# An attention and two-MLP kernel on one core: second terms of weights on VectorE, a key copy cast by its DMA, split steps by heads and earlier loads

## Chip, cores and metric

The kernel runs on one core of a Trainium2 chip. The metric is the device time of one execution in microseconds (us). Before the change the median of three runs is 738.6 us (737.14 to 741.27).

## What is computed

Attention over 2 batches, 8 heads, 576 positions and a head size of 64, with a bias that decays by the running sum of `relu(s)`; then an MLP with 2048 hidden units and a leaky ReLU; then a mixture of 4 experts with 1024 hidden units each, weighted by normalized probabilities. All of it is float32.

```python
scores = scale * (q @ k.T)
cum = cumsum(maximum(s, 0))
scores = where(causal, -1e9, scores + minimum(-(cum[i] - cum[j]), 0))
attn = softmax(scores);  x = (attn @ v) as rows of 512
x = leaky(x @ w_in) @ w_out          # 512 -> 2048 -> 512
p = probs / (sum(probs) + 1e-9)
out = sum_e p[e] * (relu(x @ w1[e]) @ w2[e])
```

## The kernel before

**Two terms.** TensorE multiplies in the type `F32R`, into which a float32 value does not fit whole. Each operand is therefore split into a first term, the value cast to `F32R` (a copy), and a second term, the value less the first (a subtraction). A product takes three matmuls: first by first, second by first, first by second. For a chunk of weights (128 x 1024) `split_w` (line 220) issues both: `nc.scalar.copy` on ACT and, right behind it, `nc.gpsimd.tensor_tensor` with `subtract` on POOL. In the profile these are `w<-raw` on ACT and on POOL.

**Stages.** Tokens fall into two sets. In the first stage (to about 225 us) attention runs as 16 units (`Unit`, line 632), one per batch and pair of heads: units 0 to 7 hold the first 256 positions of each sequence (4 items each, an item is a tile of 128 queries of one head), units 8 to 15 the rest (6 items each). From item 20 on, steps of the first MLP on the first token set are woven in (`main = mlps(phases[0])`). What is left of that MLP ends the first set (to about 250 us); the second set follows with a form of seven products (`seven_steps`, `paired_up`), and from about 373 us the experts.

**Order.** Until `fixed = False` (line 827) every instruction keeps the order in which the Python code issues it, on each engine. `attention()` (line 720) goes through the items with lags: scores of item i, exponentials of item i-1, transposes of i-3, product with the values of i-5, and, at the end of a unit, its finish of i-7. It yields at three places per item, and there the loops at lines 773 and 795 step the other generators: `main` (MLP matmuls), `units_of_w` = `supply()` and `late` = `late_splits()`. In the first half of attention two matmuls of zeros (`idling`) fill TensorE per item.

**Weights.** w_in and w_out come as 64-bit numbers. `supply()` (line 135) turns 16 chunks into float32, in six steps each: one ACT operation and four on DVE (`raw<-raw` twice, `raw<-r,raw` twice, 128 x 1024), writes the chunk to DRAM (`w_f`), and loads the next 1 MB (`r<-in_moe_...`). A chunk that TensorE needs soon is split at once; later ones are loaded again from `w_f` by `late_splits()` (line 118), which loads, yields three times, and splits.

**Keys.** For units 8 to 15 `load_keys` (line 578) loads q (`qr`, twice, for both halves of the partitions) and k (`kr`) on SP's queue; `split_keys` (line 606) makes in three steps, one per item: `qs` (ACT copy, later a DVE subtraction on 64 partitions), `ks` (ACT copy of 64 x 1152, DVE subtraction of 64 x 1152) and `kd` (a second ACT copy of the same first term, beside two rows of the decay that `decay` loads). `kd` and `ks` have two buffers each. The steps for unit 8 begin at the third item of unit 6, those of a later unit n at the third item of unit n-1. The keys of unit 8 are loaded when unit 5 is made, those of unit 9 when unit 7 is made, and of each other unit n when unit n-2 is made.

**End of a unit.** The outputs of a unit gather in `ps_o`, a PSUM pool of one buffer. At its last product DVE makes `st` and `xo` from it, and the next unit's first product has to wait for that. The flag `ending` marks a yield after which DVE shall get no step of `supply()`; it is set at the step of the exponentials only.

Of the kernel before, what the change touches and what calls it, by code (L numbers as in the profile page):

```python
# [13 lines left out]
ALU = mybir.AluOpType  # L14
# [5 lines left out]
def attention_moe_moe2(ctx: ExitStack, tc: tile.TileContext, q, k, v, s, w_in, w_out, probs, w1, w2, out):  # L20
# [10 lines left out]
    fixed = True  # L31
# [19 lines left out]
    B, H, D, S = q.shape  # L51
# [5 lines left out]
    NP = H // 2  # L57
# [17 lines left out]
    def f32(ap):  # L75
        return ap.bitcast(F32)
# [41 lines left out]
    def late_splits():  # L118

        nonlocal reading  # L120
        while len(ready) < CONVERTED:
            n = len(ready)
            if n < min(retired + WB + 2, stored):
                reading, raw = True, load_w(*stream[n][:3])
                yield
                yield
                yield
                while n >= retired + WB:
                    yield
                ready.append(split_w(raw, stream[n][1], False))  # L130
                reading = False
            else:
                yield
# [45 lines left out]
    def seven(raw):  # L179

        steps = seven_steps(raw)
        while True:
            w = next(steps)
            if w is not None:
                return w
# [34 lines left out]
    def split_w(raw, shape, paired):  # L220
        if paired:
            return seven(raw)
        w = wpool.tile([P, 2, 1024], F32R, tag="w", name="w")
        nc.scalar.copy(w[:, 0], raw)
        nc.gpsimd.tensor_tensor(w[:, 1], raw, f32(w[:, 0]), ALU.subtract)
        return w.rearrange("p l (a b) -> p l a b", a=shape[0])

    def up_piece(e, f, c):
# [340 lines left out]
    def of_unit(n):  # L569

        b = n % 2
        i0, i1 = (0, 2) if n < 2 * NP else (2, QT)
        return b, n % (2 * NP) // 2, i0, i1

    units = 4 * NP
    k_raw = {}

    def load_keys(n):

        b, hp, i0, i1 = of_unit(n)  # L580
        q0, q1 = tiles[i0][0], tiles[i1 - 1][2]
        heads = slice(2 * hp, 2 * hp + 2)
        k_of = k[b, heads, :, :q1].rearrange("h d s -> d h s")
        q_of = q[b, heads, :, q0:q1].rearrange("h d s -> d h s")
        if i0 == 0:
            nc.sync.dma_start(k_e[n % 3][:D], k_of)
            nc.sync.dma_start(q_e[n % 3][:D], q_of)
        else:
            qr = ap.tile([P, 2, S // 2 + 32], F32, tag="qr", name="qr")
            for j in range(2):  # L590
                nc.sync.dma_start(qr[j * D : (j + 1) * D], q_of)
            kr = ap.tile([P, 2, S], F32, tag="kr", name="kr")[:D]
            nc.sync.dma_start(kr, k_of)
            k_raw[n] = qr, kr
# [10 lines left out]

    def split_keys(n):

        qr, kr = k_raw.pop(n)
        qs = q_s[n % 2]
        ks, kd = (ap.tile([P, 2, S], F32R, tag=tag, name=tag) for tag in ("ks", "kd"))  # L610
        decay(n, kd)
        nc.scalar.copy(qs[:, 0], qr)
        yield
        nc.vector.tensor_tensor(qs[:D, 1], qr[:D], f32(qs[:D, 0]), ALU.subtract)
        nc.scalar.copy(ks[:D], kr)
        yield
        nc.vector.tensor_tensor(ks[D:], kr, f32(ks[:D]), ALU.subtract)
        nc.scalar.copy(kd[:D], kr)
        k_split[n] = ks, kd, qs
        yield  # L620

    def decay(n, kd):

        b, hp, i0, i1 = of_unit(n)
        q1, h = tiles[i1 - 1][2], b * H + 2 * hp
        if n < 2:
            for l, queue in enumerate((nc.sync, nc.scalar)):
                queue.dma_start(kd[D + l : D + l + 1], f32(cum2[h : h + 2, l, :q1]))
        else:
            nc.sync.dma_start(f32(kd[D:DK, :, :q1]), cum_d[:, h : h + 2, :q1])  # L630
# [84 lines left out]
    ending = False  # L715
# [4 lines left out]
    def attention():  # L720

        nonlocal ending
        items, starts, n = [], {}, 0
        i, split = 0, iter(())
        while n < units or i < len(items) + 7:
            if n < units and i == len(items):
                u = Unit(n)
                starts[n] = i
                items += [(u, *of) for of in u.items]
                if n + 2 < units and n + 2 != 2 * NP:  # L730
                    load_keys(n + 2)
                    if n + 2 < 2 * NP:
                        decay(n + 2, k_e[(n + 2) % 3])
                if n + 3 == 2 * NP:
                    load_keys(n + 3)
                n += 1
            if n < units - 1 and i == starts[n - 1] + 2:
                load_values(n + 1)
            if i == starts[n - 1] + 2 and 2 * NP - 1 <= n < units and n != 2 * NP:
                split = split_keys(max(n, 2 * NP))  # L740
            for step, lag in STEPS:
                if 0 <= i - lag < len(items):
                    u, *of = items[i - lag]
                    ending = step == Unit.exps and 0 <= i - 5 < len(items) and items[i - 5][1:] == items[i - 5][0].items[-1]
                    step(u, *of)
                if lag == 1:
                    next(split, None)
                if lag in (1, 3, 7):
                    yield i
            i += 1  # L750

# [8 lines left out]
    with ExitStack() as phase:  # L760
        x_t[0] = phase.enter_context(tc.tile_pool(name="x0pool", bufs=1)).tile([P, 2, KD, sizes[0]], F32R, name="x0")
        wpool = phase.enter_context(tc.tile_pool(name="wpool", bufs=4))
        r64p = phase.enter_context(tc.tile_pool(name="r64p", bufs=2))

        OPENED = (22, 23, 25, 27, 28, 30, 32, 34, 36)
        side, units_of_w, late, opened = attention(), supply(), late_splits(), 0
        nothing = ps_mm.tile([P, 512], F32, tag="mm", name="nothing")
        with tc.tile_pool(name="early", bufs=1) as early:
            ones = pads(early)
            cumulative()  # L770
            main = mlps(phases[0])

            for at_ in range(3 * 64):
                i = next(side)
                if done == 2 * NP:
                    break
                if at_ % 3 == 0 and i in (6, 8):
                    nc.scalar.copy(q_s[i // 2 - 3][D:DK, 1], ones[D:DK])
                if at_ % 3 == 1:
                    if i < 20:  # L780
                        idling(2)
                    elif opened < len(OPENED) and i >= OPENED[opened] and opened < 3 * (done // 2):
                        next(main)
                        opened += 1
                if at_ % 3 < 2 and i >= 31:
                    onto_held()
                if at_ % 3 == 2:
                    if i in (1, 5):
                        fetch64(i // 4)
                    if i >= 8 and (i < 21 or i >= 29):  # L790
                        next(units_of_w)
        hidden_pool(phase, 6)

        owed = 0
        for at_, i in enumerate(side):
            if at_ % 3 < 2:
                owed += WOVEN * KD / (2.0 * (48 - 6))
                while owed >= 1.0:
                    next(main)
                    owed -= 1.0  # L800
            if at_ % 3 != 1:
                next(late, None)
            if at_ % 3 == 2 or at_ % 3 == 0 and not ending:
                next(units_of_w, None)
        attn.close()
        w7pool = ctx.enter_context(tc.tile_pool(name="w7pool", bufs=2, side="right"))
        scratch = ctx.enter_context(tc.tile_pool(name="scratch", bufs=2, side="right"))
        t7pool = ctx.enter_context(tc.tile_pool(name="t7pool", bufs=1, side="right"))
        tokens = paired_steps(1, x_t[1], t7pool)
        banks.close()  # L810
        ps_mm = ctx.enter_context(tc.tile_pool(name="ps_all", bufs=8, space=PSUM))

        sevens = first_sevens()
        for m, _ in enumerate(main):
            if m % 2 == 0:
                next(late, None)
            if m % 4 == 0:
                next(tokens, None)
            if m % 4 == 2:
                next(units_of_w, None)  # L820
            if m % 4 % 2 and m >= 4:
                next(sevens, None)
        for _ in sevens:
            pass
        for _ in tokens:
            pass
    fixed = False
# [56 lines left out]
```

## Time and profile before

| | |
|---|---|
| runs shown | 738.6, 741.27, 737.14 us |
| profiled execution, its own time | 740.89 us |
| span in the trace, first to last instruction | 739.1 us |
| busy: PE, DVE, ACT, POOL | 715.3, 434.1, 330.9, 288.4 us |
| mean granted clock of TensorE | 0.998 |
| chain that ended last: PE, DVE, ACT | 88%, 5%, 3% |

In the profile, L43 is the helper that records every operation, so groups are told apart by tiles: `out<-in`. "Idle before" is time in which the engine stood still just ahead of the group, with the engine and tile that released it. PE's busy time is modelled from pipelined matmuls; PEld are its weight loads.

### The profile page before, as it was taken

How to read it: one execution, taken by the hardware profiler on the slowest of the kernel's cores; microseconds unless marked ns; L12 is line 12 of the kernel's file. 1: busy time of each engine (PE TensorE's matmuls, PEld its weight loads, DVE VectorE, ACT ScalarE, POOL GpSimd, SP SyncE). 2: the span in 40 equal slices, each digit the busy share in tenths (PEclk: the TensorE clock that was granted, in tenths of full speed). 3: DMA queues.
4: the chain of work that ended last, by engine and by line, in shares of the span. 5: the costliest groups of instructions: out<-in, count | busy, mean ns of one | idle time of the engine just before them, and what ended most of it. 6: DMA issues, size and time to landing. Idle time of an engine off the chain costs nothing.

```text
span 739.1 us, 11479 instructions
## 1 busy us (share of the span) xinstructions
PE 715.3 (97%) x4420; PEld 651.7 (88%) x4420; DVE 434.1 (59%) x866; ACT 330.9 (45%) x643; POOL 288.4 (39%) x234
## 2 busy tenths in 40 slices
PE   9988899899999999999999999999999999999997
PEld 9877788798887899999988988989889898898996
DVE  4848797889736864853874544544446444454442
ACT  5756887687654476453431322413324133132210
POOL 4111121211127969895163272422714327053200
PEclk9999999999999999999999999999999999999999
DMA  6785377675442123131020110201102011010002
GB/s 177 209 196 170 107 218 234 190 250 200 155 161 86 54 92 113 58 114 58 1 86 30 58 57 11 76 29 58 58 0 86 29 58 58 1 58 0 1 38 91
DMA packets 40745, 68.85 MB, mean 93 GB/s; under 512 B 3988, under 2 KB 22964, under 8 KB 40692
## 3 DMA queue, kind: packets, MB, share of 16 engines
q1 hardware_dynamic: 31980, 42.97, 19.2%
q10 hardware_dynamic: 8712, 25.17, 10.0%
q8 instruction: 34, 0.56, 0.3%
q14 instruction: 19, 0.16, 0.1%
HBM read 57.30 MB, written 10.82 MB: 92 GB/s over the span
## 4 chain that ended last, share of the span: by engine, by line
PE 88%; DVE 5%; ACT 3%; issue 2%; DMA 1%; SPq 0%; ACTq 0%; DVEq 0%
PE ps_d L43 40%; PE ps_u L43 34%; PE ps_o L43 5%; PE ps_sc L43 3%; PE ps_pt L43 3%; PE nothing L43 2%; DVE raw L43 2%; DMA qr<-in_q_dram 1%; DVE z L43 1%; DVE t L43 1%; PE ps_x L43 1%; ACT pv L43 1%; ACT ps_u L43 1%; ACT ks L43 0%; ACT ht L43 0%
## 5 line engine op out<-in xcount | busy, mean ns | idle before, releaser
L43 POOL TENSOR_TENSOR w<-raw,w 128x1024 fp32r<-128x1024 f32 (+2 forms) x88 | 148.1, 1701 | 399.4 <-ACT w L43 393.0
L43 PE MATMUL ps_u<-t,w 128*128 128x320 f32 (+1 forms) x1680 | 236.5, 299 | 1.2 <-DVE t L43 1.2
L43 PEld LDWEIGHTS ps_u<-t,w 128*128 128x128 f32 x1680 | 233.0, 189 | 4.9 <-DVE t L43 1.4
L43 PE MATMUL ps_d<-w,ht 128*128 128x512 f32 x864 | 203.3, 391 | 0.0
L43 PEld LDWEIGHTS ps_d<-w,ht 128*128 128x128 f32 x864 | 160.2, 188 | 31.9
L43 ACT ACTIVATE ht<-ps_u 128x320 fp32r<-128x320 f32 (+2 forms) x176 | 74.2, 433 | 156.7 <-DVE ps_u L43 128.0
L43 PE MATMUL ps_d<-ht,w 128*128 128x320 f32 (+1 forms) x576 | 109.9, 340 | 0.9 <-DVE y L43 0.9
L43 DVE SCALAR_TENSOR_TENSOR oacc<-ps_d,pn,oacc 128x512 f32<-128x512 f32 x63 | 47.3, 750 | 104.3 <-PE ps_d L43 104.3
L43 ACT CAST w<-raw 128x1024 fp32r<-128x1024 f32 (+2 forms) x88 | 64.0, 757 | 85.0 <-PE ps_d L43 69.9
L43 PEld LDWEIGHTS ps_d<-ht,w 128*128 128x128 f32 x576 | 90.8, 188 | 6.9 <-ACT t L43 1.3
L43 PEld LDWEIGHTS ps_o<-vs,pv 128*128 128x128 f32 x480 | 63.4, 192 | 11.4 <-issue 5.3
L43 DVE TENSOR_TENSOR ps_u<-ps_u,tmp 128x320 f32<-128x320 f32 (+1 forms) x120 | 56.3, 470 | 24.4 <-PE ps_u L43 22.7
L43 DVE SCALAR_TENSOR_TENSOR ht<-ps_u,ht 128x320 fp32r<-128x320 f32 (+1 forms) x128 | 56.2, 452 | 23.4 <-ACT ht L43 22.0
L43 PE MATMUL ps_o<-vs,pv 128*128 128x65 f32 x480 | 63.2, 268 | 5.1 <-issue 2.9
L43 POOL TENSOR_TENSOR w<-sums,w 128x1024 fp32r<-128x1024 f32 x24 | 59.3, 2470 | 5.1 <-ACT w L43 5.1
L43 DVE TENSOR_TENSOR tmp<-ps_u,tmp 128x320 f32<-128x320 f32 (+1 forms) x80 | 36.8, 462 | 39.6 <-PE ps_u L43 38.6
L43 PE MATMUL ps_u<-x,w 128*128 128x512 f32 x192 | 57.7, 416 | 0.0
L43 ACT ACTIVATE z<-z,mn 128x256 f32<-128x256 f32 (+4 forms) x80 | 48.6, 608 | 17.2 <-DVE mn L43 15.4
L43 DVE CUSTOM_DVE_ANT_0 z<-ps_sc,mask 128x256 f32<-128x256 f32 (+4 forms) x80 | 40.8, 511 | 20.6 <-PE ps_sc L43 14.8
L43 PE MATMUL ps_pt<-ident,z 128*128 128x128 f32 x240 | 40.2, 276 | 9.9 <-ACT pv L43 9.9
L43 ACT COPY pv<-ps_pt 128x512 f32<-128x512 f32 (+3 forms) x96 | 39.0, 423 | 19.2 <-PE ps_pt L43 18.3
L43 PEld LDWEIGHTS ps_pt<-ident,z 128*128 128x128 f32 x240 | 29.8, 141 | 18.3 <-ACT pv L43 12.0
(74 smaller groups left out, 639.1 us busy)
## 6 DMA issues: line engine op xcount, KB each, us to landing
raw<-in_moe_w_dram SPq DMA_DIRECT2D x32, 512.0 KB
raw<-w_f SPq DMA_DIRECT2D x25, 512.0 KB
r<-in_moe_w_in_dram ACTq DMA_DIRECT2D x8, 1024.0 KB
w_f<-raw ACTq DMA_DIRECT2D x16, 512.0 KB
r<-in_moe_w_out_dram ACTq DMA_DIRECT2D x8, 1024.0 KB
qr<-in_q_dram SPq DMA_DIRECT2D x16, 160.0 KB
kr<-in_k_dram SPq DMA_DIRECT2D x8, 288.0 KB
vs<-in_v_dram SPq DMA_DIRECT2D x8, 256.0 KB
```

The lines of the kernel that those rows point to most:

```text
L43: ins = call(*args, **kw)
```

## The change

1. While the order is fixed, that is to the end of the first token set, the second terms of weights are made by DVE and not by POOL, at the same place in the program.
2. `kd`'s copy of the first key term is no longer an ACT copy of `kr`: a DMA issued on POOL's queue loads it from DRAM and casts it on the way.
3. `ks` is made head by head: two ACT copies and two DVE subtractions of 64 x 576 for one each of 64 x 1152. The split has four steps in place of three, and begins with the first item of unit n-1, for unit 8 too.
4. Unit 8's keys are loaded when unit 4 is made, unit 9's when unit 6 is.
5. `late_splits` yields five times between a load and its split, for three.
6. `ending` is computed at the yields of lag 1 and lag 7, so that two places ahead of the last product of each unit get no step of `supply()`; one more step is taken at item 21.

```diff
-                yield
-                yield
-                yield
+                for _ in range(5):
+                    yield
...
-        nc.gpsimd.tensor_tensor(w[:, 1], raw, f32(w[:, 0]), ALU.subtract)
+        (nc.vector if fixed else nc.gpsimd).tensor_tensor(w[:, 1], raw, f32(w[:, 0]), ALU.subtract)
...
         decay(n, kd)
+        nc.gpsimd.dma_start(kd[:D], k[b, 2 * hp : 2 * hp + 2].rearrange("h d s -> d h s"))
         nc.scalar.copy(qs[:, 0], qr)
         yield
         nc.vector.tensor_tensor(qs[:D, 1], qr[:D], f32(qs[:D, 0]), ALU.subtract)
-        nc.scalar.copy(ks[:D], kr)
-        yield
-        nc.vector.tensor_tensor(ks[D:], kr, f32(ks[:D]), ALU.subtract)
-        nc.scalar.copy(kd[:D], kr)
+        for j in range(2):
+            nc.scalar.copy(ks[:D, j], kr[:, j])
+            yield
+            nc.vector.tensor_tensor(ks[D:, j], kr[:, j], f32(ks[:D, j]), ALU.subtract)
...
-                if n + 2 < units and n + 2 != 2 * NP:
+                if n + 2 < units and not 0 <= n + 2 - 2 * NP < 2:
                     load_keys(n + 2)
...
-                if n + 3 == 2 * NP:
-                    load_keys(n + 3)
+                if n in (2 * NP - 4, 2 * NP - 2):
+                    load_keys(n + 4 if n == 2 * NP - 4 else n + 3)
...
-            if i == starts[n - 1] + 2 and 2 * NP - 1 <= n < units and n != 2 * NP:
-                split = split_keys(max(n, 2 * NP))
+            if i == starts[n - 1] and 2 * NP <= n < units:
+                split = split_keys(n)
...
-                    ending = step == Unit.exps and 0 <= i - 5 < len(items) and items[i - 5][1:] == items[i - 5][0].items[-1]
...
+                    late = i - 5 + (lag == 7)
+                    ending = lag != 3 and 0 <= late < len(items) and items[late][1:] == items[late][0].items[-1]
                     yield i
...
-                    if i >= 8 and (i < 21 or i >= 29):
+                    if i >= 8 and (i < 22 or i >= 29):
                         next(units_of_w)
...
-            if at_ % 3 == 2 or at_ % 3 == 0 and not ending:
+            if at_ % 3 != 1 and not ending:
                 next(units_of_w, None)
```

Three places show how instructions move. TensorE's own order is the same in both.

ACT, in the first half of attention, around unit 8's first key split; before:

```order
L43 CAST qs<-qr 128x640
L43 COPY pv<-ps_pt 128x128
L43 CAST x_102<-ps_x 128x256
L43 ACTIVATE z<-z,mn 128x128
L43 CAST ks<-kr 64x1152
L43 COPY pv<-ps_pt 128x256
L43 ACTIVATE z<-z,mn 128x128
L43 CAST kd<-kr 64x1152
```

and after:

```order
L43 COPY pv<-ps_pt 128x128
L43 CAST x_102<-ps_x 128x256
L43 ACTIVATE z<-z,mn 128x128
L43 COPY pv<-ps_pt 128x256
L43 ACTIVATE z<-z,mn 128x128
L43 CAST qs<-qr 128x640
L43 COPY pv<-ps_pt 128x256
L43 ACTIVATE z<-z,mn 128x256
L43 CAST ks<-kr 64x576
L43 COPY pv<-ps_pt 128x128
L43 ACTIVATE z<-z,mn 128x256
L43 CAST ks<-kr 64x576
```

The copy `qs` stands five rows further down among the rows of attention, `ks` is in two halves an item apart, and `kd` is gone.

DVE, at the end of a unit in the second half (`st`, `RECIPROCAL` and `xo` release `ps_o`; `ISA` is the masked score with its minimum); before:

```order
L43 ISA z,mn<-ps_sc,mask 128x384
L43 ISA mn 128x1
L43 TENSOR_TENSOR ks<-kr,ks 64x1152
L43 TENSOR_SCALAR st<-ps_o 128x6
L43 RECIPROCAL st<-st 128x6
L43 TENSOR_TENSOR xo<-ps_o,st 128x384
```

and after:

```order
L43 TENSOR_TENSOR ks<-kr,ks 64x576
L43 SCALAR_TENSOR_TENSOR raw<-r_831,raw 128x1024
L43 ISA z,mn<-ps_sc,mask 128x384
L43 ISA mn 128x1
L43 TENSOR_SCALAR st<-ps_o 128x6
L43 RECIPROCAL st<-st 128x6
L43 TENSOR_TENSOR xo<-ps_o,st 128x384
```

The subtraction `ks` no longer stands between the unit's last scores and the three rows that release `ps_o`.

DVE, at the split of the first chunk of weights (`x_102` is the attention output of the first set); before:

```order
L43 TENSOR_TENSOR x_102<-ps_x,x_102 128x256
L43 ISA z,mn<-ps_sc,mask 128x128
L43 ISA mn 128x1
L43 TENSOR_SCALAR raw<-raw 128x1024
L43 ISA z,mn<-ps_sc,mask 128x256
```

and after:

```order
L43 TENSOR_TENSOR x_102<-ps_x,x_102 128x256
L43 TENSOR_TENSOR w<-raw,w 128x1024
L43 ISA z,mn<-ps_sc,mask 128x128
L43 ISA mn 128x1
L43 TENSOR_SCALAR raw<-raw 128x1024
```

The new row stands ahead of a masked score. There are 16 such rows in all; on POOL the 16 are gone and eight DMAs stand in their place.

## Rows read from the trace of the kernel before

**Rows 1.** Stretches: length, PE, PEld, DVE, ACT, POOL busy, granted clock, DMA share, GB/s.
```profile
8.00:45.00 37.00, 34.39 (x265) 31.64 (x263) 21.57 (x81) 24.67 (x60) 6.01 (x8) 1.00 0.84 229
45.00:58.00 13.00, 10.55 (x58) 8.82 (x59) 8.07 (x22) 7.88 (x18) 0.00 (x0) 0.87 0.62 141
58.00:225.00 167.00, 155.53 (x1025) 137.14 (x1024) 129.85 (x243) 123.12 (x204) 31.26 (x13) 1.00 0.57 185
225.00:739.00 514.00, 507.86 (x3037) 467.14 (x3036) 270.57 (x512) 173.13 (x359) 244.37 (x194) 1.00 0.16 52
```

**Rows 2.** Waits of PE over the whole run: total us, times, longest us.
```profile
PE ps_pt L43 <- ACT pv L43: 9.9, 7, 2.9
PE ps_o L43 <- issue: 2.9, 3, 1.3
PE ps_sc L43 <- DVE mn L43: 1.5, 3, 1.0
PE ps_o L43 <- PE ps_pt L43: 1.3, 3, 0.7
```

**Rows 3.** Chain that ended last, around 45 us: start, length, what.
```profile
36.14 9.49 DMA qr<-in_q_dram
```

**Rows 4.** Timeline at the same place, PE and ACT.
```profile
45.65 0.72 ACT L43 CAST qs<-qr 128x640 fp32r<-128x640 f32 x1 [2.88 <-DMA qr<-in_q_dram]
46.59 0.44 PE L43 MATMUL ps_pt<-ident,z 128*128 128x128 f32 x2 [2.72 <-ACT pv L43]
```

**Rows 5.** A stretch just behind it, columns as in rows 1.
```profile
47.00:50.40 3.40, 3.40 (x12) 2.72 (x11) 2.03 (x7) 3.26 (x7) 0.00 (x0) 0.50 0.72 159
```

**Rows 6.** By tile (`kd`): ns min/median/max, first and last start.
```profile
L43 PE MATMUL ps_sc<-kd,qs x64: 272/352/401, 55.8 to 206.9; 66*128 66x448 f32 x16, 66*128 66x128 f32 x16, 66*128 66x512 f32 x16, 66*128 66x384 f32 x16
```

**Rows 7.** Timeline around 86 us, ACT, then PE.
```profile
84.44 1.14 ACT L43 CAST ks<-kr 64x1152 fp32r<-64x1152 f32 x1
86.11 0.76 PE L43 MATMUL ps_pt<-ident,z 128*128 128x128 f32 x5 [1.09 <-ACT pv L43]
86.90 1.14 ACT L43 CAST kd<-kr 64x1152 fp32r<-64x1152 f32 x1
```

**Rows 8.** Timeline around 145 us: DVE, POOL, ACT, PE.
```profile
139.39 4.55 DVE L43 SCALAR_TENSOR_TENSOR raw<-r,raw 128x1024 uint32<-128x1024 uint32 x2
139.50 3.35 POOL L43 TENSOR_TENSOR w<-raw,w 128x1024 fp32r<-128x1024 f32 x1 [21.04 <-ACT w L43]
145.07 1.04 ACT L43 CAST w<-raw 128x1024 fp32r<-128x1024 f32 x1 [1.40 <-DMA raw<-w_f]
147.67 0.77 PE L43 MATMUL ps_pt<-ident,z 128*128 128x128 f32 x5 [2.91 <-ACT pv L43]
```

**Rows 9.** By tile (`kr`, `qr`, `raw` to 225 us): ns min/median/max, first and last start.
```profile
L43 DVE TENSOR_TENSOR ks<-kr,ks x8: 1351/1352/3442, 50.0 to 187.6; 64x1152 fp32r<-64x1152 f32 x8
L43 DVE TENSOR_TENSOR qs<-qr,qs x8: 809/812/815, 47.4 to 183.2; 64x640 fp32r<-64x640 f32 x8
L43 DVE TENSOR_SCALAR raw<-raw x32: 675/689/2875, 19.2 to 202.7; 128x1024 f32<-128x1024 f32 x16, 128x1024 uint32<-128x1024 uint32 x16
L43 DVE SCALAR_TENSOR_TENSOR raw<-r,raw x32: 1207/1220/3299, 22.7 to 207.8; 128x1024 uint32<-128x1024 uint32 x32
```

**Rows 10.** Timeline at the end of a unit (91 us), DVE, then PE.
```profile
89.27 1.35 DVE L43 TENSOR_TENSOR ks<-kr,ks 64x1152 fp32r<-64x1152 f32 x1
91.74 0.96 PE L43 MATMUL ps_o<-vs,pv 128*128 128x65 f32 x7 [1.30 <-issue]
```

**Rows 11.** Groups on DVE and POOL by shape, 8 to 240 us: busy us, mean ns, idle before.
```profile
L43 DVE SCALAR_TENSOR_TENSOR raw<-r,raw 128x1024 uint32<-128x1024 uint32 x32 | 42.3, 1322 | 0.3
L43 DVE TENSOR_SCALAR raw<-raw 128x1024 f32<-128x1024 f32 x16 | 17.5, 1091 | 0.1
L43 DVE TENSOR_SCALAR raw<-raw 128x1024 uint32<-128x1024 uint32 x16 | 13.7, 858 | 0.1
L43 POOL TENSOR_TENSOR w<-raw,w 128x1024 fp32r<-128x1024 f32 x16 | 40.1, 2505 | 181.4 <-ACT w L43 175.1 <-PE ps_pt L43 6.3
```

More of the change, by code (lines that the diff above doesn't have):

```diff
@@ L606, in split_keys @@
     def split_keys(n):
+        b, hp = of_unit(n)[:2]
         qr, kr = k_raw.pop(n)
```

## The prediction

> **What bounds the kernel now.** I read the busy times by stretch first [rows 1]. From 225 us on PE is busy 507.9 us of 514, 99%; there nothing but less PE work would help, and PE's order is the same in both kernels. PE stands still in attention: 11.5 us of 167 between 58 and 225 us, 2.5 of 13 between 45 and 58 us. From 8 to 45 us it is kept busy with zeros, so that stretch can lengthen but not shorten. In attention no other engine is full: DVE is busy 129.9 of 167 us, ACT 123.1. What PE waits for is therefore lateness of single instructions on engines that work in order, and the next view, PE's waits, says which [rows 2]: ACT's copy `pv` 9.9 us in 7 waits, `ps_o` 2.9 us in 3 (put down to "issue"; the timeline below shows DVE behind it), and two kinds of 1.5 and 1.3 us. These 15.6 us, and what the clock adds, are all that the change can win.
>
> **A, the late load of q.** The chain shows a DMA of `qr` that takes 9.49 us to land, and behind it ACT's copy `qs` [rows 3]. ACT stands still 2.88 us for it, and PE 2.72 us for the `pv` that stands behind it on ACT [rows 4]. PE had stood still nearly 3 us, and for the next 3.40 us its granted clock is 0.50, that is 1.2 GHz [rows 5]. Of 3.40 us at half the clock, 1.7 are lost. The change issues this load a unit earlier on SP (ahead of unit 5's values, which move behind it) and asks for `qs` a unit later. Eight units take the 48 us from 8 to 55.8 us, where `kd` is first used [rows 6], so 6 us each; between load and copy now lie about three units, 18 us, over 9.49. I take both: 2.7 + 1.7 = **-4.4 us**. If only the wait went and the clock fell all the same, it would be -2.7.
>
> **B, ACT's copies of keys.** Around 86 us ACT runs without a pause; `ks` takes 1.14 us just ahead of the `pv` that PE waits 1.09 us for, and `kd` another 1.14 us ahead of the next [rows 7]. The change takes away `kd` (8 x 1.14 = 9.1 us of ACT), cuts `ks` in halves an item apart, and moves all of it two items forward. Of the 9.9 us of `pv` waits, 2.7 belong to A and 2.9 to C; 4.3 are left. At most all go, at least none (ACT has other work in the same places: evictions, conversions, the same copies `w`). I take three quarters, since the relief per unit, 1.14 us and half of another 1.14, is larger than each of these waits but one: **-3.2 us**.
>
> **C, the wait at 147.7 us.** Two things meet there [rows 8]. Two DVE operations that take 1.22 us each [rows 9] take 4.55 us together, while POOL's subtraction, in the same stretch, takes 3.35 us; DVE and POOL hold each other up. And ACT stands still 1.40 us for a chunk that is still on its way from `w_f`. PE waits 2.91 us. The change takes POOL's 16 subtractions away from here, and gives the load five yields for three, an item more: eight units of six items take 151 us [rows 6], so 3.1 us an item. Both causes go: **-2.9 us**.
>
> **D, the release of `ps_o`.** At the end of a unit DVE does `ks`, 1.35 us, and only then `st` and `xo`; PE waits 1.30 us [rows 10]. All three waits of this kind [rows 2] have that row ahead of `st`. In the new order it stands elsewhere, and `ending` keeps conversion steps away from the same place. **-2.9 us**; at least -1.5, if a conversion step in the third place (lag 3) does the same now and then.
>
> **E, the 16 subtractions on DVE.** No row shows this operation on DVE. By the same subtraction of 640 and of 1152 columns, 0.812 and 1.352 us [rows 9], a column costs 1.05 ns and 1024 columns 1.22 us. So DVE gets 16 x 1.22 = 19.5 us more. It gets back what POOL took from it: `raw<-raw` 31.2 us where 32 x 0.689 = 22.0 would do, `raw<-r,raw` 42.3 for 39.0 [rows 9, 11], and `ks` one operation of 3.44 us for 1.35: together 14.6 us. DVE thus has nearly the same sum of work, but the new operation stands right behind ACT's cast of 1.04 us [rows 8], for which POOL could wait at no cost and DVE, with the masked scores queued behind, cannot. What of it does PE pay? Best case nothing, as DVE has some 37 us of slack in the main stretch [rows 1]. Worst case all of the operation and the cast, 16 x (1.22 + 1.04) = 36.2 us. The nearest row is the loss that DVE has now: 14.6 us of blocking cost PE the 2.91 us of C, a fifth. A fifth of 19.5 is **+3.9 us**. The first two of them, at about 29 and 37 us, stand in the stretch with the zeros, where PE cannot catch up.
>
> **At nothing.** The eight DMAs of `kd` (288 KB each): POOL has nothing else to do then. The first two have no wait ahead of them and go out early; the others wait on POOL's queue for the scores of the unit two before, and have a unit of 18.9 us [rows 6] to land; the slowest landing that I have is 9.49 us [rows 3]. Their bounds are 0 and the cost of a late one, below. They add 2.4 MB to the 41 that move from 8 to 225 us, at a DMA share of 0.57 to 0.84 [rows 1]. The Trainium skill ("DMA: Bandwidth & Descriptors", Anatomy of one DMA) gives 2.0 us and bytes over 436 GB/s for a DMA from this queue, by which 288 KB would be an estimated 2.7 us; no row here shows it. The halved `ks` on both engines add one start each, under 0.1 us, eight times. The decay's load now waits on SP for the same scores, with values and chunks queued behind it that are due an item or more later. The end of the first set gets its last chunk by DVE in 1.22 us where POOL took 2.5 [rows 11], behind a slower cadence of loads: no change.
>
> **The sum.** -4.4 - 3.2 - 2.9 - 2.9 + 3.9 = -9.5 us. Against the profiled execution's own 740.9 us that is 731.4; that execution lies 2.3 us above the median of the runs, so against the median it is **729.1 us**.
>
> **Rivals.** *E costs nothing*: DVE's slack covers it, and all of B goes: -4.4 - 4.3 - 2.9 - 2.9 = -14.5, 724.1 us. For it: the DVE total hardly changes. Against: it waits in order.
> *The waits come back elsewhere*: once `pv` and `ps_o` are early, the masked scores are late; half of B, C and D returns (-4.5) and E costs twice its fifth (+7.8): -1.1, 737.5 us. For it: DVE at 78% and ACT at 74% beside a PE that never stops have little room.
> *Load order helps little*: `qr` still lands late behind values and 1 MB chunks at a DMA share of 0.84; A is halved and more, 733.5 us.
> *Slower by DVE*: DVE waits for ACT's cast at most splits, ACT for DVE's scores, and PE for both. Of the 36.2 us half falls on PE, +18.1 against the -13.4 of A to D: +4.7, 743.3 us. It decides from a share of 37% on, and from 47% the loss passes 0.5%. For it: each split puts 2.3 us ahead of masked scores that now come an item, 3.1 us, apart. Against: the same engine stood 4.55 us in one place and PE lost 2.9.
> *Slower by `kd`*: DVE's `raw<-raw`, 0.69 us for 1024 columns where `raw<-r,raw` takes 1.22 [rows 9], may hold POOL up as DVE held POOL at 139.5 us, a microsecond [rows 8]; were POOL's DMAs so delayed as to land after a unit's start, six units would each pay what `qr` did, 4.4 us: 755 us. It needs over 9 us of delay, 18.9 less 9.49, where the row shows one. The Trainium skill ("SBUF — State Buffer", SBUF: two separate sides) says that a DMA issued from this queue starves of descriptors while VectorE runs an operation on both of its ports; that rule speaks against this part of the change. What hangs on it: by the rule alone each DMA would be late by the 0.69 us of one such operation, far inside the unit.
>
> **How the numbers follow.** A measurement of this kernel can tell about 0.5%, 3.7 us, from no change: faster is below 734.9, slower above 742.3. The forecast gets 0.45 (726 to 734), E at nothing 0.17, the load order 0.09, waits that come back 0.15, slower by DVE 0.11, slower by `kd` 0.03. The first three make 0.71, less 0.05 for a forecast case that falls just short: faster 0.66, same 0.20, slower 0.14. The range reaches from just below the second case to above the fourth, 723 to 740, and leaves out the slower cases and a little below.
>
> **What would show it.** Right: no `qs` wait and a full clock near 47 us; no `ps_o` waits under "issue"; `raw<-raw` near 0.69 us throughout; `w<-raw` on DVE near 1.22 us; PE's waits in attention from 15.6 us to some 8, now on `mn`. Wrong: DVE idle released by ACT's `w`, PE waiting for `mn` more than it waited for `pv`, or any wait of PE's for `kd`.

## The result and the profile after

| | before | after |
|---|---|---|
| median of the runs | 740.13 us (6 runs, 737.14 to 743.06) | 730.75 us (6 runs, 728.7 to 733.36) |
| ratio, 95% interval | | 0.9878 [0.9844, 0.9912] |
| profiled execution, its own time | 740.89 us | 728.7 us |
| span in the trace | 739.1 us | 726.9 us |

The change takes 9.4 us off; the forecast was 9.5 (729.1 us). The profiled execution before lies 0.8 us above its median, that of after 2.1 below, so the traces show 12.2 us between them, and some 3 of these are scatter.

Stretches of the profile after, columns as in [rows 1]:

```profile
8.00:45.00 37.00, 33.72 (x254) 30.65 (x253) 23.55 (x82) 25.02 (x60) 2.56 (x8) 1.00 0.99 259
45.00:58.00 13.00, 11.32 (x78) 9.64 (x77) 10.22 (x31) 9.21 (x22) 0.00 (x0) 1.00 0.46 110
58.00:225.00 167.00, 164.07 (x1060) 144.39 (x1060) 138.32 (x268) 117.31 (x206) 10.21 (x13) 1.00 0.63 198
```

The clock is full in all three; the fall at 47 us is gone. PE stands still 2.9 us of the 167 where it stood still 11.5. The first stretch did not get better: PE is busy 33.72 us for 34.39, and the DMA engines are busy almost throughout (0.99 for 0.84).

PE's waits over the whole run after the change (total us, times, longest), which answer to [rows 2]:

```profile
PE ps_sc L43 <- DVE mn L43: 2.5, 5, 0.7
...
PE ps_x L43 <- ACT pv L43: 0.8, 1, 0.8
...
PE ps_o L43 <- PE ps_pt L43: 0.7, 2, 0.4
...
PE ps_o L43 <- DVE xo L43: 0.6, 1, 0.6
...
PE ps_pt L43 <- ACT pv L43: 0.4, 1, 0.4
...
PE ps_o L43 <- issue: 0.2, 1, 0.2
```

The waits of `ps_pt` for `pv` fell from 9.9 to 0.4 us, those of `ps_o` under "issue" from 2.9 to 0.2; the masked scores (`mn`) rose from 1.5 to 2.5, now the largest.

By tile, after, to 225 us (ns min/median/max, first and last start), answering to [rows 9]:

```profile
L43 DVE TENSOR_SCALAR raw<-raw x32: 678/690/696, 18.7 to 202.0; 128x1024 f32<-128x1024 f32 x16, 128x1024 uint32<-128x1024 uint32 x16
...
L43 DVE SCALAR_TENSOR_TENSOR raw<-r,raw x32: 1210/1220/1227, 22.2 to 204.9; 128x1024 uint32<-128x1024 uint32 x32
...
L43 DVE TENSOR_TENSOR w<-raw,w x16: 1215/1224/3426, 28.3 to 224.0; 128x1024 fp32r<-128x1024 f32 x16
```

No conversion step is held up any more: the longest `raw<-raw` takes 0.70 us for 2.87, the longest `raw<-r,raw` 1.23 for 3.30. The subtraction takes 1.22 us, as worked out from the columns; one of 16 takes 3.43, at 224 us, where POOL has begun a subtraction of its own.

**By stretch.** PE runs the same instructions in the same order in both kernels, so its own rows mark the stretches: the first half from PE's first score (8.44 us before, 7.91 after) to its first one of unit 8, the second half from there to the wait of PE that marks the end of attention (226.07 us before, 214.52 after), and the rest, each kernel's one profile. PE's first score of unit 8, before, then after:

```profile
55.51 0.45 PE L43 MATMUL ps_sc<-ks,qs 128*128 128x448 f32 x1
...
52.68 0.45 PE L43 MATMUL ps_sc<-ks,qs 128*128 128x448 f32 x1
```

| kernel | first half | second half | rest |
|---|---|---|---|
| before | 47.1 | 170.6 | 513.0 |
| after | 44.8 | 161.8 | 512.4 |
| forecast of the difference | -4.4 and the first two of E (0.5) | -9.0 and the rest of E (3.4) | 0 |
| measured | -2.3 | -8.7 | -0.6 |

The total was right, the parts were not: the first half gained 1.6 us less than forecast, the second 3.1 more. The experiments ask why.

### The profile page after: what moved, and what is told of

It reads as the page before. It is cut to its first block, busy times and chain, and to the rows that moved or that the text cites. A ratio compares the mean times of both kernels' runs of the same rounds, so it can differ in the third digit from the quotient of the medians.

```text
span 726.9 us, 11487 instructions
## 1 busy us (share of the span) xinstructions
PE 712.8 (98%) x4420; PEld 650.1 (89%) x4420; DVE 440.6 (61%) x890; ACT 323.1 (44%) x643; POOL 253.2 (35%) x226
## 4 chain that ended last, share of the span: by engine, by line
PE 88%; DMA 3%; DVE 3%; ACT 2%; issue 1%; POOL 1%; SPq 0%; ACTq 0%; POOLq 0%; DVEq 0%
PE ps_d L43 41%; PE ps_u L43 36%; PE ps_o L43 6%; PE ps_sc L43 3%; PE ps_pt L43 3%; DMA vs<-in_v_dram 1%; DMA kr<-in_k_dram 1%; ACT z L43 1%; DMA ke<-cum_d 1%; DVE t L43 1%; DVE w L43 1%; PE ps_x L43 1%; ACT w L43 0%; SPq L43 0%; DVE z L43 0%
## 5 line engine op out<-in xcount | busy, mean ns | idle before, releaser
L43 POOL TENSOR_TENSOR w<-raw,w 128x512 fp32r<-128x512 f32 (+2 forms) x72 | 108.8, 1533 | 218.6 <-ACT w L43 218.5
L43 DVE SCALAR_TENSOR_TENSOR oacc<-ps_d,pn,oacc 128x512 f32<-128x512 f32 x63 | 47.3, 751 | 104.3 <-PE ps_d L43 104.3
L43 POOL TENSOR_TENSOR sums<-raw 128x256 f32<-128x256 f32 x48 | 37.6, 801 | 56.1 <-ACT t L43 54.6
L43 POOL DMA_DIRECT2D kd<-in_k_dram x8 | 4.8, 601 | 145.3 <-PE ps_sc L43 126.4
```

The source lines that it names most:

```text
L43: ins = call(*args, **kw)
```

## The experiments

Every kernel here was timed in five rounds beside the kernel before, whose medians were 739.93 us for the first four, 738.43 for the next four and 739.46 for the last four. Two kernels of different groups are compared by their ratios; their intervals reach about 2 to 3 us to either side, so a difference of that size between two of them is not settled by the times alone.

### The subtractions back on POOL (e1_pool)

```diff
-        (nc.vector if fixed else nc.gpsimd).tensor_tensor(w[:, 1], raw, f32(w[:, 0]), ALU.subtract)
+        nc.gpsimd.tensor_tensor(w[:, 1], raw, f32(w[:, 0]), ALU.subtract)
```

> The change with one part undone: the 16 second terms of weights go back to POOL; all else stays. My theory (E cost PE little in the main stretch and mostly at the first two, in the stretch with the zeros; POOL's blocking cost PE 2.9 us in C): PE's waits on DVE's mn and xo near 30 us (0.63 and 0.64 us) vanish, raw<-raw on DVE is up to 2.9 us again in places, one or two PE waits of 1 to 3 us come back between 58 and 225 us; time 1 to 3 us above the change, about 732 to 734 where the change has 730.8. Rival (the 16 subtractions cost PE the +3.9 us of E all along the stage, and C was the late chunk alone): 2 to 4 us below the change, about 727 to 729.

733.24 us, 0.9911 [0.988, 0.9941]: 2.4 us above the change by the ratios, with intervals that overlap, and in no case the 3.9 below it that E's charge would give back. The timeline shows what POOL does to DVE, and PE's wait ten us later:

```profile
132.33 5.59 POOL L43 TENSOR_TENSOR w<-raw,w 128x1024 fp32r<-128x1024 f32 x2 [9.82 <-ACT w L43]
...
132.91 5.56 DVE L43 TENSOR_SCALAR raw<-raw 128x1024 f32<-128x1024 f32 x2
...
142.11 0.16 DVE L43 TENSOR_SCALAR st<-ps_o 128x6 f32<-128x6 f32 x1
...
143.19 1.30 PE L43 MATMUL ps_o<-vs,pv 128*128 128x65 f32 x10 [1.41 <-issue]
```

Two `raw<-raw` of 0.69 us take 5.56 while POOL's two subtractions run. From there to `st` DVE has no pause, and PE waits 1.41 us for it; then its clock is 0.50 for 3.4 us. So the blocking costs PE something in this order of work too, in another place than [rows 8].

### kd as an ACT copy again (e2_kd_act)

```diff
-        nc.gpsimd.dma_start(kd[:D], k[b, 2 * hp : 2 * hp + 2].rearrange("h d s -> d h s"))
...
+        nc.scalar.copy(kd[:D], kr)
```

> The change with one part undone: kd is an ACT copy of kr again (64 x 1152, 1.15 us, as the last step of the split), with no DMA on POOL's queue. My theory (B: ACT's relief is worth some 3 us in the main stretch; the two early DMAs crowd the first 45 us a little): +1 to +3 us against the change, 732 to 734, with PE waits on ACT pv back to 2 to 4 us in sum. Rival (the moved start and the halved ks did B's work, kd was hidden, and the early DMAs at a DMA share of 0.99 cost the first stretch about a microsecond): 0 to -2 us, 729 to 731.

730.5 us, 0.9872 [0.9835, 0.9909]: no loss shows, as the rival said, though the intervals leave room for one of 2 or 3 us. ACT has its 8 copies of 1.14 us back. In the profile the waits of `ps_pt` for `pv` are 2.8 us for the change's 0.4, but at the end of attention only 0.7 us of that are left. Taking `kd` off ACT was worth nothing that shows once the split had its new place.

### Splits of units 9 to 15 at the old place (e3_late_start)

```diff
-            if i == starts[n - 1] and 2 * NP <= n < units:
+            if i == starts[n - 1] + (2 if n > 2 * NP else 0) and 2 * NP <= n < units:
```

> The change with the split of units 9 to 15 beginning at the third item of the unit before, as it did before the change; unit 8's split, the halves and kd's DMA stay. Half of ks (0.75 us) then stands just ahead of st and xo again. My theory (D: it is this row ahead of st that held ps_o, 2.9 us for 1.35): PE waits on ps_o put down to issue come back with 0.2 to 0.7 us at three to six unit ends, and ACT is crowded later in the unit; +1.5 to +3 us, 732 to 734. Rival (D came from the ending rule alone): within 0.5 us of the change.

733.56 us, 0.9918 [0.9888, 0.9947]: 3.0 us above the change by the ratios; the intervals overlap. That is the time that was expected, but not by the expected waits: `ps_o` under "issue" has one of 0.3 us, not three to six. Between the two profiles 2.8 us are lost by the end of attention, 1.2 of them at a wait near 22 us, before this edit can act. It is the direction of B and D, but less than e7_start_alone shows for the same place in the kernel before.

### The old loads of units 8 and 9 (e4_loads)

```diff
-                if n + 2 < units and not 0 <= n + 2 - 2 * NP < 2:
+                if n + 2 < units and n + 2 != 2 * NP:
...
-                if n in (2 * NP - 4, 2 * NP - 2):
-                    load_keys(n + 4 if n == 2 * NP - 4 else n + 3)
+                if n + 3 == 2 * NP:
+                    load_keys(n + 3)
```

> The change with the loads of units 8 and 9 where they were (unit 8's made with unit 5, unit 9's with unit 7); unit 8's split still begins a unit later than before the change. My theory of A as predicted (the early load is needed): qs waits for qr again, PE stands still 1 to 3 us near 47 us, the clock may fall again; +2 to +4 us, 733 to 735. Rival (moving the split by itself gives the load its time: issued near 35 us and landed 9.5 us later it is there at 45, and qs is asked for at 47): within 0.5 us of the change, and the values of unit 5 come earlier.

730.99 us, 0.9877 [0.9839, 0.9915]: no difference shows, as the rival said, and `qs` does not wait for `qr`. Loading sooner has no part in the gain that shows.

### Only the split of unit 8 later, from before (e5_q_alone)

```diff
-            if i == starts[n - 1] + 2 and 2 * NP - 1 <= n < units and n != 2 * NP:
-                split = split_keys(max(n, 2 * NP))
+            if i == starts[n - 1] + (0 if n == 2 * NP else 2) and 2 * NP <= n < units:
+                split = split_keys(n)
```

> The kernel before with one thing moved: unit 8's split begins with the first item of unit 7, not with the third of unit 6; loads, copies and POOL's subtractions stay as before. My theory (A is a matter of when qs is asked for, since the change kept its gain with the old loads): the wait for qr and the 3.4 us at half the clock go, -3.5 to -4.5 us against the kernel before, a ratio of 0.994 to 0.995. Rival (the wait has cover further on: PE comes earlier to unit 8 and waits there): under -1.5 us, a ratio over 0.998.

737.06 us, 0.9977 [0.995, 1.0003]: 1.7 us less by the ratio, and the expected 3.5 to 4.5 lie at the interval's edge or outside it; the expectation was missed. In the profile the price of A is met in its own stretch: the first half takes 42.3 us for 47.1, 4.8 less. The second half then takes 172.7 for 170.6, with a wait at 142.6 us and a clock of 0.50 for 3.4 us behind it, where the kernel before kept its clock.

### Only the subtractions on DVE, from before (e6_dve_alone)

```diff
-        nc.gpsimd.tensor_tensor(w[:, 1], raw, f32(w[:, 0]), ALU.subtract)
+        (nc.vector if fixed else nc.gpsimd).tensor_tensor(w[:, 1], raw, f32(w[:, 0]), ALU.subtract)
```

> The kernel before with the 16 second terms of weights on DVE, nothing else. My theory (undoing this alone in the change cost 2.5 us; POOL's blocking of DVE costs PE more than the subtractions do): -1 to -4 us against the kernel before, a ratio of 0.995 to 0.999, with raw<-raw at 0.69 us throughout and the 2.9 us wait at 148 us gone. Rival (it pays only with the split's ACT copies out of the way, since DVE now waits for ACT's cast): 0 to +4 us, a ratio of 1.000 to 1.005.

739.24 us, 1.0008 [0.9982, 1.0034]. A loss of 3.9 us would be 1.0053, outside the interval, and so would be a gain of C's 2.9; the expected gain was missed and the rival met. The wait of [rows 8] is still there, with no POOL subtraction near it. ACT in this kernel, and the matmul that waits:

```profile
141.56 1.02 ACT L43 CAST w<-raw 128x1024 fp32r<-128x1024 f32 x1
...
142.50 1.13 ACT L43 ACTIVATE raw<-r 128x1024 f32<-128x1024 f32 x1
...
143.53 0.72 ACT L43 COPY pv<-ps_pt 128x512 f32<-128x512 f32 x2
...
144.14 1.03 PE L43 MATMUL ps_pt<-ident,z 128*128 128x128 f32 x5 [2.75 <-ACT pv L43]
```

ACT does not wait for the chunk here. What stands ahead of `pv` is the cast `w` of one generator and the conversion step `raw<-r` of another, back to back, 2.1 us. In the trace of before the same two rows stand ahead of `pv` as well: 1.04 us at 145.07 [rows 8] and 1.12 us behind it; there ACT's 1.40 us for the chunk come on top.

Another wait is gone here, at which no edit was aimed. The split of unit 8 stands where it stood before, with the same loads, and yet `qs` starts without a pause, where it had waited 2.88 us [rows 4]:

```profile
43.86 0.71 ACT L43 CAST qs<-qr 128x640 fp32r<-128x640 f32 x1
```

So the wait of A hangs on when that load lands, and not every execution need have it.

### Only the place of all splits, from before (e7_start_alone)

```diff
-            if i == starts[n - 1] + 2 and 2 * NP - 1 <= n < units and n != 2 * NP:
-                split = split_keys(max(n, 2 * NP))
+            if i == starts[n - 1] and 2 * NP <= n < units:
+                split = split_keys(n)
```

> The kernel before with all splits begun with the first item of the unit before (unit 8's too), in the old three steps with whole copies, kd by ACT and POOL's subtractions. My theory (the place of the split does A, D and what is real of B): -6 to -8 us against the kernel before, a ratio of 0.989 to 0.992, with no wait for qr and no ps_o waits put down to issue. Rival (D needs the halves, or the ending rule): -3.5 to -4.5 us, what A gives alone.

731.45 us, 0.9898 [0.9865, 0.9932]: about 7.5 of the change's 9 us, with two lines. Against e5_q_alone, units 9 to 15 alone bring 5.6 us. PE's waits in its profile:

```profile
PE ps_pt L43 <- ACT pv L43: 3.5, 3, 1.9
...
PE ps_sc L43 <- DVE mn L43: 1.9, 3, 1.0
...
PE ps_o L43 <- DVE xo L43: 1.3, 2, 0.7
```

Both kinds that bounded the kernel before fell at once: `pv` from 9.9 to 3.5 us, `ps_o` under "issue" from 2.9 to none, with 1.3 us on `xo`. The longest `pv` wait, at 137.5 us, is again behind `w` and `raw<-r`.

### The first two subtractions on POOL, old loads (e8_first_pool)

```diff
-        (nc.vector if fixed else nc.gpsimd).tensor_tensor(w[:, 1], raw, f32(w[:, 0]), ALU.subtract)
+        (nc.vector if fixed and len(ready) >= 2 else nc.gpsimd).tensor_tensor(w[:, 1], raw, f32(w[:, 0]), ALU.subtract)
```

The loads are as in e4_loads.

> The change with the first two second terms back on POOL (the other 14 on DVE) and the loads of units 8 and 9 where they were before. My theory (the first two cost PE 0.63 + 0.64 us near 30 us and about 0.8 near 40 us, where PE is kept busy with zeros and cannot catch up; the early key load costs 0.8 us at 40 us): 1 to 2 us below the change, about 729. Rival (what is won there is lost again at unit 8, whose inputs set its start): within 0.5 us of the change.

729.42 us, 0.9865 [0.9824, 0.9905]: the profile of this kernel has a wait that no other one has.

```profile
54.27 0.71 PE L43 MATMUL ps_sc<-kd,qs 66*128 66x448 f32 x1 [3.77 <-DMA kd<-cum_d]
```

The decay's rows of unit 8 landed 7.7 us after their issue, and PE stood still for them, with its clock at 0.50 for 6.8 us. Up to that wait it was ahead: its first half took 42.4 us for the change's 44.8, and for the 45.6 of e4_loads, from which it differs by the first two subtractions alone.

### Place and subtractions together, from before (f1_start_dve), and with the first two on POOL (f4_start_dve14)

Both are e7_start_alone with one line more, that of e6_dve_alone for f1_start_dve, that of e8_first_pool for f4_start_dve14.

> The kernel before with two things: all splits begin with the first item of the unit before, and the 16 second terms of weights are on DVE; whole copies of ks, kd by ACT, old loads, three yields, old ending rule. My theory now (the place of the split carries the change, DVE's subtractions add some 2 us once it stands there, the other four parts add nothing that shows): a ratio of 0.986 to 0.990, as the change has, 0.9878. Rival (the others matter: the late chunk's wait near 140 us, 2 to 3 us with the clock's drop behind it, comes back without the five yields): 0.990 to 0.993.

> As f1_start_dve, but with the first two second terms on POOL, where they were before the change. My theory (the first two on DVE cost 1.3 to 2 us in the stretch with the zeros): 1 to 2 us below f1_start_dve. Rival (no difference: what unit 8 waits for sets its start): within 0.7 us of it.

731.5 us, 0.9897 [0.9873, 0.9921], and 730.63, 0.988 [0.9856, 0.9903]. On top of the place alone (0.9898) the 16 subtractions make no difference that shows in the time. The first two cost some 0.9 us by the medians, less than these intervals can tell; by the profiles the first half takes 44.1 us with them on DVE and 42.3 with them on POOL. Both have the wait of C, here in f1_start_dve:

```profile
137.94 1.03 ACT L43 CAST w<-raw 128x1024 fp32r<-128x1024 f32 x1
...
138.87 1.16 ACT L43 ACTIVATE raw<-r 128x1024 f32<-128x1024 f32 x1
...
139.91 0.59 ACT L43 COPY pv<-ps_pt 128x512 f32<-128x512 f32 x1
...
140.55 1.33 PE L43 MATMUL ps_pt<-ident,z 128*128 128x128 f32 x5 [2.59 <-ACT pv L43]
```

The same pair, on time and without a pause. With this wait (1.9 to 2.8 us) and the clock that falls at it, the second halves of e7_start_alone, f1_start_dve and f4_start_dve14 take 165.7, 165.4 and 165.7 us; the change's takes 161.8. The fall is not in every execution: four of f1_start_dve's six runs have a mean clock of 1.000, its profiled run 0.998.

### The old rule for the end of a unit, three yields (f3_ending_yields)

```diff
-                for _ in range(5):
+                for _ in range(3):
...
+                    ending = step == Unit.exps and 0 <= i - 5 < len(items) and items[i - 5][1:] == items[i - 5][0].items[-1]
...
-                    late = i - 5 + (lag == 7)
-                    ending = lag != 3 and 0 <= late < len(items) and items[late][1:] == items[late][0].items[-1]
...
-            if at_ % 3 != 1 and not ending:
+            if at_ % 3 == 2 or at_ % 3 == 0 and not ending:
```

> The change with two parts undone together: the old ending rule and three yields between a late load and its split. My theory (neither shows once the split begins early; C's cause in ACT's wait for the chunk comes back in part): +0 to +2 us against the change, a ratio of 0.988 to 0.990. Rival (C and D rest on these two, as predicted in part): +3 to +5 us, 0.992 to 0.995, with waits of 1 to 3 us near 140 us and ps_o waits.

735.81 us, 0.9946 [0.9919, 0.9973], an interval that lies apart from the change's: about 5 us are lost, as the rival said, and more than by any other part that was taken back. DVE and PE at the end of unit 9:

```profile
83.58 2.48 DVE L43 SCALAR_TENSOR_TENSOR raw<-r,raw 128x1024 uint32<-128x1024 uint32 x2
...
85.99 0.55 DVE L43 CUSTOM_DVE_ANT_0 z<-ps_sc,mask 128x384 f32<-128x384 f32 x1
...
86.46 0.16 DVE L43 TENSOR_SCALAR st<-ps_o 128x6 f32<-128x6 f32 x1
...
86.88 0.56 DVE L43 TENSOR_TENSOR xo<-ps_o,st 128x384 f32<-128x384 f32 x1
...
87.54 1.30 PE L43 MATMUL ps_o<-vs,pv 128*128 128x65 f32 x10 [1.49 <-issue]
```

and the stretch behind it, columns as in [rows 1]:

```profile
89.40:92.80 3.40, 3.40 (x12) 2.72 (x12) 2.88 (x7) 1.05 (x2) 0.00 (x0) 0.50 0.99 360
```

Two conversion steps stand where `ks` stood [rows 10], and hold `st` and `xo` back; the wait takes the clock with it, 1.49 and another 1.7 us. The wait near 140 us that the rival named, though, is 0.36 us here, with three yields: `raw<-r` runs at 137.62 and `w` at 140.95, with the exponentials between them.

### Old loads, kd on ACT, the first two on POOL (f2_first_pool_act)

This is e8_first_pool with the edit of e2_kd_act.

> The change with the first two second terms on POOL, kd by ACT for all units, and the old loads for units 8 and 9. My theory (the first stretch, unit 0's first scores to unit 8's, is as short as with the split moved alone, 43.7 us for 47.3, and the main stretch stays at the change's 158.5 to 160): a ratio of 0.982 to 0.985. Rival (the loads of unit 8 land late behind the 1 MB chunks, as the decay rows did with kd by DMA, and PE waits 2 to 4 us at unit 8): 0.986 to 0.989.

727.09 us (4 runs, 726.83 to 728.43), 0.9836 [0.9812, 0.986]: the fastest kernel of the study by its median, some 3.1 us below the change by the ratios; the two intervals still overlap. Its stretches:

```profile
8.00:45.00 37.00, 35.52 (x272) 32.74 (x272) 22.82 (x86) 26.52 (x66) 6.01 (x8) 1.00 0.84 238
45.00:58.00 13.00, 11.57 (x77) 9.73 (x76) 11.56 (x31) 10.77 (x22) 0.00 (x0) 1.00 0.73 183
58.00:225.00 167.00, 162.43 (x1051) 143.76 (x1051) 137.65 (x263) 123.21 (x211) 8.38 (x8) 1.00 0.57 183
```

PE is busy 35.52 us of the first 37 where the change has 33.72, at a DMA share of 0.84 for 0.99. The halves take 42.2 and 162.6 us for the change's 44.8 and 161.8: three parts of the change that bring nothing that shows are out, and the first half is as short as in e7_start_alone. (The expectation counts from DVE's first masked score to its first of unit 8; so counted, the halves are 44.8 and 159.3 us here, 47.3 and 158.5 in the change.)

## Why the prediction was right in the sum and wrong in its parts

**The sum.** -9.4 against -9.5 us is in part luck. The sum was made from one profile, and between the two profiles the change took 12.2 us off, 11.0 of them in attention: 2.3 in the first half, where 3.9 were forecast, and 8.7 in the second, where 5.6 were. That second half lies nearer to the first rival (E costs nothing: B's 4.3, C's 2.9 and D's 2.9 make 10.1). What makes 9.4 of the 12.2 is that the traced execution before was slower than its median and the one after faster.

**A, right in the trace, smaller in the time, then half eaten.** In the profiles the wait, the clock and the size are shown by e5_q_alone and e7_start_alone, whose first halves take 42.3 and 42.2 us for 47.1. In the time e5_q_alone brought 1.7 us, and 4.4 (a ratio of 0.994) lies outside its interval. The forecast took the wait of the traced execution for that of every one; e6_dve_alone has none with the same loads and the same place. Two items, half a unit, are what `qs` was moved by, not "a unit later"; and the load was not the remedy (e4_loads).

The steps that failed in this stretch are the first two of E, put at 0.5 us, and the earlier load, put at no cost. Up to 40 us, row by row of PE, the change falls 2.2 us behind the kernel before. The timeline of the change shows where:

```profile
28.34 1.23 DVE L43 TENSOR_TENSOR w<-raw,w 128x1024 fp32r<-128x1024 f32 x1 [0.65 <-ACT w L43]
...
29.83 0.70 PE L43 MATMUL ps_sc<-ke,qe 128*128 128x256 f32 x2 [0.63 <-DVE mn L43]
...
31.73 0.52 PE L43 MATMUL ps_o<-vs,pv 128*128 128x65 f32 x3 [0.64 <-DVE xo L43]
...
38.40 1.23 DVE L43 TENSOR_TENSOR w<-raw,w 128x1024 fp32r<-128x1024 f32 x1 [1.30 <-ACT w L43]
...
39.34 0.51 ACT L43 ACTIVATE z<-z,mn 128x256 f32<-128x256 f32 x1 [0.97 <-DMA kr<-in_k_dram]
...
40.06 0.44 PE L43 MATMUL ps_x<-ident,xo 128*128 128x128 f32 x2 [0.75 <-ACT pv L43]
```

DVE waits 0.65 and 1.30 us for the cast, then subtracts for 1.23. Behind the first of these PE's score and product wait 0.63 and 0.64 us, which puts PE 1.4 us behind. At 39 us ACT stands still 0.97 us, which the trace puts down to the landing of the early key load, and PE waits 0.75 us for its `pv`: another 0.8. This last wait is not the subtraction's, for with POOL's subtractions and the early loads (e1_pool) it is longer:

```profile
38.91 0.51 ACT L43 ACTIVATE z<-z,mn 128x256 f32<-128x256 f32 x1 [2.09 <-DMA kr<-in_k_dram]
...
39.62 0.44 PE L43 MATMUL ps_x<-ident,xo 128*128 128x128 f32 x2 [1.68 <-ACT pv L43]
```

All five profiles with the early loads have this wait (PE 0.47 to 1.68 us), none of the nine with the old ones. The two near 30 us are the subtraction's: the seven profiles with the first two on POOL have no PE wait over 0.11 us at these places, the seven with them on DVE wait 0.31 to 0.63 and 0.64 us. By pairs that differ in the first two alone they cost 1.8 us of the first half (f1_start_dve less f4_start_dve14) and 3.3 (e4_loads less e8_first_pool, where 1.3 arise at 17 us, before the first subtraction). One profile of each stands behind these numbers; no time settles them.

**B, too small, and for the wrong reason.** All but 0.4 us of the `ps_pt` waits for `pv` went, not three quarters. But taking away `kd`, "9.1 us of ACT", was worth nothing that shows in the time (e2_kd_act). The place of the splits did it, as e7_start_alone shows: it still has both copies whole, and its units 9 to 15 bring 5.6 us, B's and D's forecasts together being 6.1. The halves of `ks`, put "under 0.1 us", cost DVE 0.15 us each time (twice 0.75 us for 1.35), 1.2 us in all.

**C, right in size, wrong in cause.** "Both causes go" named POOL's blocking and a late chunk. e6_dve_alone has neither at that place, and the wait is 2.75 us. What stands there in every profile that has the wait (before, e5_q_alone, e6_dve_alone, e7_start_alone, f1_start_dve, f4_start_dve14) is the cast `w` and the conversion step `raw<-r` on ACT in one gap ahead of `pv`. In the change they lie ten us apart, and PE has no wait there:

```profile
132.01 1.06 ACT L43 CAST w<-raw 128x1024 fp32r<-128x1024 f32 x1
...
136.83 0.75 ACT L43 COPY pv<-ps_pt 128x512 f32<-128x512 f32 x2
...
138.97 0.73 ACT L43 COPY pv<-ps_pt 128x512 f32<-128x512 f32 x2
...
141.69 1.14 ACT L43 ACTIVATE raw<-r 128x1024 f32<-128x1024 f32 x1
```

Which edit parts them was not tried by itself, so this cause is read from the traces; f3_ending_yields parts them with three yields and the old rule, so neither the two further yields nor the new rule is needed for it.

**D, right.** `ps_o` under "issue" went from 2.9 to 0.2 us. The place takes `ks` away (e7_start_alone), and with the rest of the change in, the old rule and three yields bring a wait of 1.49 us back, with two conversion steps ahead of `st`. The two edits were undone together; that the rule is the one is read from the trace, not shown apart.

**E, mis-sized.** "A fifth" of 19.5 us, +3.9, was charged over the whole stage. Measured: 0.6 us (interval -1.3 to 2.5) alone, nothing that shows on top of the place (f1_start_dve beside e7_start_alone), and in the full change a gain of 2.4 that the intervals leave open (e1_pool). DVE did wait for ACT's `w`, 8.3 us in 8 waits, which the prediction had as a sign of being wrong; DVE's slack in the second half took it, since the waits of PE for `mn` rose by 1.0 us only. The work that came to DVE (19.5 us) was largely paid by the blocking that went (14.6).

**The other rivals.** Waits came back as the second rival says, but only 1.0 us more on `mn` (1.5 to 2.5) and 0.8 on `ps_x`; those on `xo` stayed (0.7, now 0.6). The early loads brought nothing that shows (e4_loads). Nothing speaks for DVE as the bound. For `kd` by DMA, the trace of the change gives this, by tile (ns min/median/max; then us to landing):

```profile
L43 POOL DMA_DIRECT2D kd<-in_k_dram x8: 578/581/746, 9.4 to 159.0; - x8
...
DMA to landing us min/median/max: 3.6/5.0/9.6
```

Every one landed before its unit began, and PE never waited for it. The Trainium skill ("SBUF — State Buffer", SBUF: two separate sides) has such DMAs starve of descriptors while VectorE runs an operation on both of its ports; no late one shows here, and whether a part of the 9.6 us is that, no run tells. The fixed cost and rate of the Trainium skill ("DMA: Bandwidth & Descriptors", Anatomy of one DMA) made an estimated 2.7 us; the trace, with other transfers under way, has a median of 5.0.

## What to carry to other kernels

Before pricing copies and engines, ask which rows of two independent generators meet in front of the instruction that is waited for: moving a step by two items (two lines) brought most of this change, taking work away from the same engine nothing that shows. Split a forecast by stretch as well as by mechanism, because a gain in one and a loss in another can make a right sum for wrong reasons. Mark such stretches by the engine that bounds the kernel: counted by DVE's scores the first half seems to gain 0.9 us, by PE's it gains 2.3. And undo each part of a change that gained: three of these parts brought nothing that shows or cost a little, and the kernel without them has the lowest median.

## What the runs showed of the hardware

**A lost wait can cost twice.** After PE had stood still, its granted clock was at 0.50 (1.2 GHz) for 3.4 us, 1.7 us lost, in most kernels: around the waits of 2.72 us (before, at 47 us), 2.12 (e5_q_alone), 1.95 (e7_start_alone), 2.59 (f1_start_dve), 2.81 (f4_start_dve14), 2.75 (e6_dve_alone), 1.49 (f3_ending_yields) and 1.41 (e1_pool); after 3.77 us it was 6.8 us (e8_first_pool). But the wait of 2.91 us in the kernel before [rows 8] had no fall behind it, nor had 1.41 us at 79.7 us in f1_start_dve. The profiles of the change, e2_kd_act, e3_late_start, e4_loads and f2_first_pool_act show no fall in attention. Nor does one kernel fall alike in every execution: the 53 runs of the kernel before beside the experiments have mean clocks of 0.989 to 1.000, 16 of them 0.999 or more, and all six runs of the change have 0.999 or 1.000. What is missing from 1, times the span, is an estimate of what the clock cost in a run: 2.0 to 3.2 us in the mean of each group of runs before, 0.2 in that of the change. By that estimate 2 to 3 of the 9.4 us are the clock's.

**DVE and POOL.** `raw<-raw` was stretched from 0.69 to 2.9 us beside POOL's subtraction, `ks` halves from 0.75 to 2.86 (e1_pool); with POOL quiet the spread of 32 such operations is 0.02 us.

**An early load can hold up another engine.** In the change the chain of waits has the SP load of `kr`, issued at 30.38 us and 8.47 us under way, and behind its landing a DMA issue of ACT (38.87 us) and the late exponential at 39.34. The issue of the same 1 MB load with the early loads, in the change, and with the old ones, in e4_loads:

```profile
38.87 0.37 ACTq L43 DMA_DIRECT2D r<-in_moe_w_out_dram  x1
...
37.65 0.42 ACTq L43 DMA_DIRECT2D r<-in_moe_w_out_dram  x1
```

In the five profiles with the early loads it stands at 38.4 to 41.2 us, and ACT's exponential behind it waits 0.92 to 2.09 us; in the nine with the old loads it stands at 35.0 to 37.7 us and no such wait follows. Why an issue on ACT's queue follows that landing, the traces do not tell; the load itself is asked for much later.
